# Decaying attention and two feed-forward layers: two more jobs through the DMA crossbar, merged scale passes, and a new order of the first loads

## The chip, the cores and the metric

The kernel runs on one core of one Trainium2 chip. The metric is the device time of one execution in microseconds, as the median of several runs.

## The reference, cut to what matters

```python
# q, k, v: 4 x 8 x 576 x 64; f: 4 x 8 x 576
scores = q @ k.T / 8
cum    = cumsum(log(clip(f, 1e-4, 1)))
attn   = softmax(where(causal, scores + cum[i] - cum[j], -1e9))
x = (attn @ v) as 2304 tokens x 512
h = x @ w_in;  x = (h * sigmoid(h)) @ w_out        # 512 -> 2048 -> 512
h = x @ w2_in; out = (h * cos(h)) @ w2_out         # 512 -> 2048 -> 512
```

All of it is float32.

## The kernel before

**The work.** The 32 heads go in 16 pairs, n = 0 to 15. Each pair has a job "a" for its first 256 rows and a job "b" for its last 320 (`ORDER`). A job "a" is one unit, c01, and a job "b" is three: c3, c2 and T. A unit makes scores on TensorE (PE), subtracts the maximum on VectorE (DVE), takes the exponential on ScalarE (ACT), normalises, transposes the probabilities, and multiplies them by the values (`pv_tasks`).

**Two ways to transpose.** In `unit_tasks` and `pv_tasks` a job "b" takes one of two ways by `BY_DMA`. With False, PE transposes float32 blocks (line 810, the narrow one line 813), ACT copies them from PSUM, and the product is float32 (line 948). With True, the probabilities are split into a high and a low fp16 part (`eh`, line 834 for the low one), six DMA transposes write them to `pt` (lines 841 and 844), the values are split too (line 700), and the product is three fp16 passes (line 937). Before the change this is True for 0 to 5, 6, 8, 10, 12 and 14: eleven jobs.

**Decays.** Logarithms are taken and summed once (`d_ln`, `d_scan`, lines 448 to 452). Jobs "a" with n < 4 add them on PE by a matmul (`f_dk`, line 768); the others read them back from DRAM, spread over the partitions.

**The two layers.** Tokens go in nine groups of 256 (j = 0 to 8) and hidden columns in eight pairs p. A step (l, j, p) is a product into `h` (line 1329; for the first group line 1318), elementwise work that leaves g, and a product into `y` (line 1441 in layer 1, line 1220 in layer 2). In layer 1, groups 0 and 1 take the output weights as float32. From group 2 (`J16`) on they are fp16 pairs, which need a scale for each p (`scale_tasks` with kind "o"), and g is made with `rg3`, the result of `f_v1` (line 1044). Layer 2 is fp16 pairs throughout. Its weights are converted while layer 1 runs and go through DRAM; `f_v` makes its factors.

**A scale.** The squares of a tile are summed by ACT (`squares`, line 358), added by DVE (`f_add`, line 425), summed over the partitions by a matmul with ones (line 429), and turned into a power of two and its inverse by three DVE passes (lines 434 to 436). For q and k of a job "b" the same is done in `balance` (lines 593 to 596).

**The order.** A planner (`Scheduler`) runs a model of the engines while the program is built. At each moment an engine takes the ready task with the lowest key whose buffers (`TOK`) are free, and issues it; so every engine gets a fixed list. Layer steps have keys from -1000 and go first. Jobs "a" have keys 0 to 50 or so, jobs "b" follow, six to a job. The first layer's weights have keys 10 to 60, the squares and scales of its output weights `C16 + C161 * p`, the second layer's weights `C2K0 + C2K1 * i`; their loads wait for step `W2N0 + W2N1 * i`. `KO` adds an offset by the kind of task. While the model finds PE idle in the first 60 us, it puts fillers into PE's list (line 410). All loads are issued from SyncE (SP), in the planned order; `QD` and `LOOK` set how far loads run ahead.

Of the kernel before, what the change touches and what calls it, by code (L numbers as in the profile page):

```python
# [29 lines left out]
BY_DMA = [n < 6 or n % 2 == 0 for n in range(NP)]  # L30
# [25 lines left out]
KO = {"gs": 1.5, "g2": 1.5, "gl2": 1.5, "cb2": 0.5, "cb3": 0.5, "chi": -2.5, "g": -5.5}  # L56
HAM = 3.4133
# [3 lines left out]
EXTRA = {"DVE": 1.2, "POOL": 0.8}  # L61
# [7 lines left out]
KDEC, KDP = 12.0, -0.5  # L69
# [10 lines left out]
class Scheduler:  # L80
# [35 lines left out]
    def run(self):  # L116
# [56 lines left out]
        while events:  # L173
# [23 lines left out]
            while progress:  # L197
                progress = False
                for e in ENG:
# [41 lines left out]
                    if e == "PE":  # L241
                        w = int(now / HAM)
                        while win < w:
                            warm = work[win] > 0.7 * HAM
                            win += 1
                            if len(work) <= win:
                                work.append(0.0)
                        if not warm:
                            end += best.dur
                        a = now  # L250
                        while a < end - 1e-9:
                            w = int(a / HAM + 1e-9)
# [58 lines left out]
def c_dma(mb):  # L311
    return 0.01 + mb / 0.41
# [3 lines left out]
def decay_attention_silu_cos_kernel(ctx, tc, qa, qb, f, w1i, w1o, w2i, w2o, out):  # L316
# [81 lines left out]
    qe = sb.tile([128, 4], I32, name="qe")  # L398
# [20 lines left out]
    def scale_tasks(i, deps, key, top=15, turns=None):  # L419


        cell = {}

        def f_add():
            nc.vector.scalar_tensor_tensor(sq16[:, i:i + 1], sq[:, 0, i:i + 1], 2.0 ** -60, sq[:, 1, i:i + 1], ALU.max, ALU.add)

        def f_sum():
            cell["n"] = ps.tile([128, 512], F32, tag="s", bufs=TOK["s"], name="nrm")
            nc.tensor.matmul(cell["n"][:, 0:1], ones16, sq16[:, i:i + 1], start=True, stop=True, skip_group_check=True)

        def f_two():
            n = cell["n"][:, 0:1].bitcast(I32)
            a, b = scl[:, i:i + 1].bitcast(I32), inv[:, i:i + 1].bitcast(I32)
            nc.vector.tensor_scalar(b, n, 1, 0x3F800000, ALU.logical_shift_right, ALU.bitwise_and)  # L434
# [4 lines left out]
        t = add("DVE", 0.1, f_add, deps, key=key, name="sc")  # L439
        t = add("PE", 0.04, f_sum, [t], key=key - 10000.0, acq=["s"], name="sc")  # L440
        return add("DVE", 0.46, f_two, [t], key=key, rel=["s"], name="sc")
# [5 lines left out]
    def d_ln():  # L447
        nc.vector.tensor_scalar(fc[0:32, 0:S], fc[0:32, 0:S], 1e-4, 1.0, ALU.max, ALU.min)

    def d_scan():  # L450
        nc.vector.tensor_tensor_scan(cum[0:32, 0:S], ones[0:32, 0:S], lf[0:32, 0:S], 0.0, ALU.mult, ALU.add)
        nc.vector.tensor_scalar(cum[0:32, 0:S], cum[0:32, 0:S], -8.0, None, ALU.mult)
# [52 lines left out]
    for i in range(2 * NF):  # L505
# [5 lines left out]
        def load(c=c, kind=kind, src=src):  # L511
# [5 lines left out]
                         [decay] if kind == "o" and c >= NF - NT_ else [], kind == "o")  # L517
# [37 lines left out]
    def load_tasks(jb, u):  # L555
# [5 lines left out]
        def tile_of(tag):  # L561
            n, dt = {"qk": (QK, F32), "v": (QB - RB, F32), "dk": (QB, F32)}[tag]
            if beta:
                return sbt(tag, [128, n], dt, name=tag)
            if not half:
                pairs[tag, jb.n // 2] = sbt(tag, [128, n], dt, name=tag)
            return pairs[tag, jb.n // 2]
# [36 lines left out]
        def norm():  # L604
            jb.qn = ps.tile([128, 512], F32, tag="s", bufs=TOK["s"], name="nrm")
            nc.tensor.matmul(jb.qn[:, 0:nq], ones16, qn.bitcast(BF16).rearrange("p n (c t) -> p n c t", t=2)[:, jb.n, 0:nq, 1], start=True, stop=True, skip_group_check=True)
# [45 lines left out]
        own = beta or not half  # L652
        t0 = add("SP", 0.5, load, key=u, acq=["qs"] if beta else ["qk"] if own else [],
                 deps=[] if own else [jb.mate.loads[2]], dma=c_dma(0.49 if beta else 0.26), name="ldq")
        tv = add("SP", 0.5, load_v, key=u + 0.1, acq=["v"] if own else [], deps=[] if own else [jb.mate.loads[0]],
# [47 lines left out]
        if not beta and jb.n < NS_:  # L703
            if half:
                values.append([tv, jb.mate.loads[0]])
            jb.loads, jb.masked = [tv, tv, t0], {"c01": [masked]}
            return [tl]
        t1 = add("SP", 0.5, decays, [decay] + ([] if own else [jb.mate.loads[1]]), key=u, acq=["dk"] if own else [],
                 dma=1.3 if beta else 1.1, name="ldd")
        jb.loads = [tv, t1, t0]  # L710
# [334 lines left out]
    factors1 = add("DVE", 0.9, f_v1, sc1 + [wready[1, "i", 2 * p][0] for p in range(NPR)], key=-500, name="sc")  # L1045
# [4 lines left out]
    for i in range(2 * NF):  # L1050
# [17 lines left out]
        ts = scale_tasks(k, [halves[c - 1][2], halves[c][2]], key, *((15, by) if kind == "i" else (14,)))  # L1068
# [45 lines left out]
    factors2 = add("DVE", 0.6, f_v, sc2, key=-500, name="sc")  # L1114
# [47 lines left out]
    def factor_tasks(l, j, ts, key):  # L1162
# [20 lines left out]
        if j < 2:  # L1183
            return [add("DVE", 0.1, f1(p, p + 1), [ts, wts[p]], key=key, name="sc") for p in range(NPR)]
        t = add("DVE", 0.1, f1(0, NPR), [ts] + wts, key=key, name="sc")
# [331 lines left out]
```

## Time and profile before

| | |
|---|---|
| median of 3 runs | 912.09 us (912.05 to 913.18) |
| profiled execution | 911.74 us, of which the span of instructions is 909.9 |
| PE busy | 899.1 us, 99% |
| DVE, ACT, POOL busy | 760.6, 694.9, 160.7 us |
| mean granted TensorE clock | 0.996 |

POOL is GpSimd. An engine's busy time counts its own instructions; a matmul's time in the trace includes its way through the array, so that single matmuls overlap. The chain of waits gives each piece of time to one instruction only, and is the better view of what PE's work costs.

### The profile page before, as it was taken

The page shows a single profiled execution, that of the slowest core. Times are in us where ns is not written, and L with a number is a line of the kernel's source. Part 1 is how long each engine was busy: PE and PEld are TensorE (multiplying, and loading weights), DVE is VectorE, ACT ScalarE, POOL GpSimd, SP SyncE. Part 2 cuts the span into 40 slices and gives each one's busy share as a digit, 9 for nine tenths or more (in the row PEclk, how much of TensorE's full clock was granted, in tenths as well). Part 3 has the DMA queues.
Part 4 walks back from the last instruction along what each step waited for, and adds up shares of the span by engine and source line. Part 5 has one row for each costly group of instructions (what it writes and reads, how often), then busy time and mean ns, then how long its engine had stood idle before and what let it go on. Part 6 is the DMA issues. An engine that isn't in the chain of part 4 may idle for free.

```text
span 909.9 us, 20973 instructions
## 1 busy us (share of the span) xinstructions
PE 899.1 (99%) x7928; PEld 753.0 (83%) x7928; DVE 760.6 (84%) x1854; ACT 694.9 (76%) x1425; POOL 160.7 (18%) x236
## 2 busy tenths in 40 slices
PE   9999999999999999999999999999999999999997
PEld 5667777788887888887888888888888888888886
DVE  6899878987876999988899987888888888787775
ACT  7999999876868888788797767766676666666663
POOL 6652321133212324323120100000000000000000
PEclk9999999999999999999999999999999999999999
DMA  8965744967987878886674997000001000000010
GB/s 318 372 223 160 235 151 82 196 142 162 202 191 204 213 215 209 209 191 177 221 233 157 317 355 237 24 24 24 24 24 48 24 24 24 1 25 24 1 24 24
DMA packets 113701, 130.03 MB, mean 143 GB/s; under 512 B 63872, under 2 KB 76160, under 8 KB 113600
## 3 DMA queue, kind: packets, MB, share of 16 engines
q1 hardware_dynamic: 113600, 128.70, 49.2%
q8 instruction: 62, 1.02, 0.5%
q14 instruction: 39, 0.32, 0.1%
HBM read 90.25 MB, written 24.72 MB: 126 GB/s over the span
## 4 chain that ended last, share of the span: by engine, by line
PE 93%; ACT 3%; DVE 2%; DMA 1%; issue 1%; DVEq 0%; ACTq 0%; SPq 0%
PE h L1329 40%; PE y L1441 20%; PE y L1220 18%; PE pv L948 2%; PE spin L410 2%; PE st L762 2%; PE tt L810 2%; PE pv L937 2%; PE st L755 1%; ACT junk L358 1%; PE st L743 1%; PE st L768 1%; DMA rw<-w1i 1%; PE st L742 1%; PE h L1318 0%
## 5 line engine op out<-in xcount | busy, mean ns | idle before, releaser
L1329 PE MATMUL h<-x,wi 128*128 128x256 f16 x3432 | 404.6, 273 | 0.0
L1329 PEld LDWEIGHTS <-wi 128*128 128x128 f16 x3432 | 331.6, 98 | 46.6 <-issue 6.5
L1441 PE MATMUL y<-g,rw 128*128 128x256 f16 (+1 forms) x1600 | 224.1, 292 | 2.7 <-ACT g L333 2.7
L1220 PE MATMUL y<-wo,g 128*128 128x256 f16 x1512 | 176.5, 273 | 0.0
L1220 PEld LDWEIGHTS <-g 128*128 128x128 f16 x1512 | 147.9, 98 | 17.1
L1441 PEld LDWEIGHTS <-rw 128*128 128x128 f16 x1344 | 129.2, 98 | 18.3 <-issue 3.3
L793 ACT ACTIVATE e<-e,su 128x128 f32<-128x128 f32 (+4 forms) x144 | 82.9, 578 | 14.4 <-DVE su L772 14.2
L1383 ACT ACTIVATE t<-h,ru 128x512 f32<-128x512 f32 x72 | 49.2, 684 | 57.8 <-PE h L1329 57.5
L1408 DVE TENSOR_TENSOR g<-t,g 128x896 f16<-128x896 f32 x72 | 78.4, 1089 | 14.9 <-ACT g L1405 13.1
L1405 ACT ACTIVATE g<-t 128x896 f16<-128x896 f32 x72 | 68.0, 944 | 28.8 <-DVE t L1399 28.7
L1393 DVE SCALAR_TENSOR_TENSOR t<-h,rg,t 128x512 f32<-128x512 f32 x72 | 54.0, 749 | 34.7 <-ACT t L1390 34.7
L1389 ACT ACTIVATE t<-t,ru 128x512 f32<-128x512 f32 x72 | 51.7, 717 | 26.7 <-DVE t L1386 26.7
L1354 ACT ACTIVATE t<-h,rg 128x512 f32<-128x512 f32 x72 | 48.9, 680 | 29.3 <-PE h L1329 28.9
L333 ACT ACTIVATE g<-t,rg 128x512 f16<-128x512 f32 (+1 forms) x72 | 51.6, 716 | 22.2 <-PE y L1441 19.4
L772 DVE CUSTOM_DVE_ANT_0 e<-st,dk 128x256 f32<-128x256 f32 (+3 forms) x128 | 59.2, 492 | 8.4 <-PE st L762 3.3
L1386 DVE SCALAR_TENSOR_TENSOR t<-t,ru,h 128x512 f32<-128x512 f32 x72 | 53.5, 743 | 8.9 <-ACT t L1383 8.9
L1357 DVE SCALAR_TENSOR_TENSOR t<-t,h 128x512 f32<-128x512 f32 x72 | 49.2, 683 | 11.9 <-ACT t L1354 11.6
L1441 PEld LDWEIGHTS y<-g,rw 128*128 128x128 f32 x256 | 47.0, 194 | 13.1 <-ACT g L333 3.9
L353 DVE SCALAR_TENSOR_TENSOR g<-t,rg,g 128x512 f16<-128x512 f32 x56 | 43.3, 773 | 13.4 <-ACT g L333 12.8
L1390 ACT ACTIVATE t<-t,halfpi 128x512 f32<-128x512 f32 x72 | 52.0, 722 | 2.3
L834 DVE SCALAR_TENSOR_TENSOR eh<-e,su,eh 128x512 f16<-128x512 f32 (+1 forms) x66 | 41.6, 657 | 1.1 <-ACT eh L333 0.6
L333 ACT ACTIVATE e<-e,su 128x256 f32<-128x256 f32 (+4 forms) x78 | 35.2, 509 | 0.9 <-DVE inv L434 0.5
(158 smaller groups left out, 1260.7 us busy)
## 6 DMA issues: line engine op xcount, KB each, us to landing
rw<-w1i SPq DMA_DIRECT2D x16, 512.0 KB, 5.4
rw<-w1o SPq DMA_DIRECT2D x16, 512.0 KB, 7.3
x<-x_d SPq DMA_DIRECT2D x16, 512.0 KB, 4.2
dk<-decay_d SPq DMA_DIRECT2D x16, 512.0 KB, 4.9
raw<-w2i SPq DMA_DIRECT2D x16, 512.0 KB, 5.0
raw<-w2o SPq DMA_DIRECT2D x16, 512.0 KB, 4.2
qs<-qb SPq DMA_DIRECT2D x16, 480.0 KB, 4.2
w2o_d<-w SPq DMA_DIRECT2D x24, 256.0 KB, 3.3
```

The lines of the kernel that those rows point to most:

```text
L333: nc.scalar.activation(dst, src, AF.Copy, scale=scale)
L772: nc.vector.tensor_tensor_reduce(out, s, d, -0.125, first, ALU.add, ALU.min, cell["sm"][:, o:o + 1])
L793: nc.scalar.activation(x, x, AF.Exp, bias=sm[:, i:i + 1], scale=-1.0, accum_out=sm[:, 4 + i:5 + i])
L1220: nc.tensor.matmul(y[bank][:, 256 * half:256 * half + 256], g[:, gi, ga], w[:, wi, 256 * col:256 * col + 256], start=p == 0 and half == 0 ...
L1329: nc.tensor.matmul(h[:, i], w[:, wi, 128 * k:128 * k + 128], x[:, xi, k], start=(i == 0 and q == 0 and k == 0), stop=(i == 1 and q == 2 an ...
L1386: nc.vector.scalar_tensor_tensor(cell["t"], cell["t"], r, cell["h"], ALU.subtract, ALU.subtract)
L1389: nc.scalar.activation(cell["t"], cell["t"], AF.Abs, scale=r)
L1390: nc.scalar.activation(cell["t"], cell["t"], AF.Sin, scale=-2.0 * PI, bias=halfpi)
L1393: nc.vector.scalar_tensor_tensor(cell["t"], cell["h"], r, cell["t"], ALU.mult, ALU.mult)
L1405: nc.scalar.activation(g_t[s][:, 0], cell["w"], AF.Copy)
L1408: nc.vector.tensor_tensor(g_t[s][:, 1], cell["w"], g_t[s][:, 0], ALU.subtract)
L1441: nc.tensor.matmul(y[:, e * TB:(e + 1) * TB], w[:, wi, 128 * ec:128 * ec + 128], g[:, gi, i * TB:(i + 1) * TB], start=(st and e == 0), sto ...
```

## The change

Two more jobs "b", 7 and 9, take the way through the crossbar. The scales of the first layer's output weights are made for four p at once, and some inverses are made later, all eight of a kind in one pass. `balance` has two passes instead of three; its sum on PE writes the two norms twice. The decays are summed in two parts, and the four matmuls of line 768 wait for the first alone. The loads of a job "a" wait only for the buffer of their pair, and no longer for the load of its other half. `GAPB` puts the jobs "b" 12 key units later, `LEAD` their loads 3 before, `USTEP` their three units 1 apart and not 2. Many constants of the planner have new values.

```diff
-BY_DMA = [n < 6 or n % 2 == 0 for n in range(NP)]
+BY_DMA = [n < 11 or n % 2 == 0 for n in range(NP)]
-LOOK = 12
+LOOK = 14
-QD = 3
+QD = 1.5
-CK2 = 12
+CK2 = 6
-GAP4, GAP8 = 8, 12
+GAP4, GAP8 = 6, 12
-C2K0, C2K1 = 150, 0.5
-W2N0, W2N1 = 30, 1.0
-J16, C16, C161 = 2, 70, 2.0
+C2K0, C2K1 = 160, 0.2
+W2N0, W2N1 = 35, 0.9
+J16, C16, C161 = 2, 90.0, 4
-KO = {"gs": 1.5, "g2": 1.5, "gl2": 1.5, "cb2": 0.5, "cb3": 0.5, "chi": -2.5, "g": -5.5}
-HAM = 3.4133
+KO = {"gs": 0.5, "g2": 1.5, "gl2": 1.5, "cb2": 2.0, "cb3": 0.0, "chi": 2, "g": -8, "max": -0.5, "ldq": 1.0, "exp": -0.5, "xc": -2.0, "nm": 0.0, "rec": -4, "clo": -1.0, "ws": -2.0, "qhi": -1.5, "sqw": -2.5, "cb1": 4, "ldd": -3.0, "hide": -1.0, "tc": 1.5, "vhi": 3.5, "cexp": 0.5}
+HAM, HAM0 = 3.4133, 1.3
-EXTRA = {"DVE": 1.2, "POOL": 0.8}
+EXTRA = {"DVE": 1.2, "POOL": 1.4}
-KDEC, KDP = 12.0, -0.5
+KDEC, KDP = 14, -1
+LEAD, USTEP, GAPB = 3, 1, 12
...
+    def inverse(i, n, top):
+        b = inv[:, i:i + n].bitcast(I32)
+        nc.vector.tensor_scalar(b, b, 1.0, float((65 - top) << 23), ALU.mult, ALU.add)
-    def scale_tasks(i, deps, key, top=15, turns=None):
+    def scale_tasks(i, deps, key, top=15, turns=None, n=1, late=False):
...
-            nc.vector.tensor_scalar(b, b, 1.0, float((65 - top) << 23), ALU.mult, ALU.add)
+            if not late:
+                inverse(i, n, top)
...
+    def d_scan(a, b):
+        def f():
+            nc.vector.tensor_tensor_scan(tot[0:32, a:b], ones[0:32, a:b], lf[0:32, a:b],
+                                         tot[0:32, a - 1:a] if a else 0.0, ALU.mult, ALU.add)
+            nc.vector.tensor_scalar(cum[0:32, a:b], tot[0:32, a:b], -8.0, None, ALU.mult)
+        return f
...
+    d1 = add("DVE", 0.45, d_ln(0, 256), [d0], key=-100)
+    d2 = add("ACT", 0.4, d_log(0, 256), [d1], key=-100)
+    d1 = add("DVE", 0.55, d_ln(256, S), [d1], key=-99)
+    scanned = add("DVE", 0.9, d_scan(0, 256), [d2, dm, dz], key=-100)
+    d2 = add("ACT", 0.5, d_log(256, S), [d1, d2], key=-100)
...
+    d3 = add("DVE", 1.15, d_scan(256, S), [d2, scanned], key=-99)
-    scanned = d3
...
+            nc.vector.scalar_tensor_tensor(qsc[:, :, n].bitcast(I32), qe[:, 1:nq + 1:nq - 1], float(127 << 23), qe[:, 0:2],
+                                           ALU.add, ALU.subtract)
...
-        t0 = add("SP", 0.5, load, key=u, acq=["qs"] if beta else ["qk"] if own else [],
-                 deps=[] if own else [jb.mate.loads[2]], dma=c_dma(0.49 if beta else 0.26), name="ldq")
+        at = {}
+        if not beta:
+            at = jb.mate.at if half else {tag: add("SP", 0.0, lambda: None, key=u - 300, acq=[tag], name="at")
+                                          for tag in (["qk", "v", "dk"] if jb.n >= NS_ else ["qk", "v"])}
+            jb.at = at
+        t0 = add("SP", 0.5, load, key=u, acq=["qs"] if beta else [], deps=[] if beta else [at["qk"]],
+                 dma=c_dma(0.49 if beta else 0.26), name="ldq")
...
-            sp = load_tasks(jb, pos)
+            if kind == "b" and jb.n == 0:
+                pos += GAPB
+            sp = load_tasks(jb, pos - (LEAD if kind == "b" else 0))
...
-                    un += unit_tasks(jb, u, pos + 2 * i, sp, [])
+                    un += unit_tasks(jb, u, pos + USTEP * i, sp, [])
...
+    NQ = 4
...
+        if p % NQ == 0:
+            q = [add(**squares(lambda c=c: wo32[c]["w"], 512, sq[:, c % 2, k + c // 2 - p:k + c // 2 - p + 1]),
+                     deps=wready[1, "o", c], key=C16 + C161 * (c // 2), name="sqw") for c in range(2 * p, 2 * p + 2 * NQ)]
+            ts = scale_tasks(k, q, C16 + C161 * (p + NQ - 1), 14, n=NQ, late=True)
+            sc1.append(ts)
...
+        inverse(o, NPR, 14)
...
+        inverse(i, NPR, 15)
+        inverse(o, NPR, 14)
```

## Rows read from the trace of the kernel before

In the groups of instructions a row has the line, engine and operation, out<-in and the count, then busy us, mean ns of one, and idle us of the engine before them with what ended it. A timeline row has its start and length in us, then the same, and in brackets the idle time before it. In rows 1 a stretch and its length stand first, then the busy time of PE, PEld (its weight loads), DVE, ACT and POOL, each with its count of instructions, the granted clock as a share of 2.4 GHz, the mean busy share of the DMA engines, and GB/s.

**Rows 1.** Busy time of each engine, TensorE's granted clock and DMA, by stretch.

```profile
0.00:60.00 60.00, 58.94 (x380) 37.03 (x381) 47.47 (x143) 52.87 (x155) 39.70 (x55) 1.00 0.91 330
60.00:75.00 15.00, 11.33 (x70) 8.56 (x69) 14.41 (x40) 14.87 (x41) 3.91 (x5) 0.89 0.53 161
75.00:200.00 125.00, 125.00 (x942) 98.50 (x940) 107.70 (x337) 114.50 (x296) 30.45 (x46) 1.00 0.63 159
200.00:440.00 240.00, 240.00 (x2289) 195.11 (x2288) 204.99 (x555) 193.61 (x434) 71.35 (x113) 1.00 0.79 195
440.00:560.00 120.00, 119.59 (x1102) 105.72 (x1101) 102.14 (x240) 90.77 (x177) 15.30 (x19) 1.00 0.79 269
```

**Rows 2.** Groups of TensorE matmuls: fillers, and the sums of squares.

```profile
L410 PE MATMUL spin<-ones 128*128 128x512 bf16 x89 | 24.3, 410 | 1.1 <-DVE ones L372 1.1
...
L429 PE MATMUL nrm<-sq,ones 128*128 128x1 bf16 x50 | 8.4, 168 | 1.4 <-DVE inv L434 1.0 <-DVE sq L425 0.3
```

**Rows 3.** Chain of waits, start and length of each piece in us.

```profile
1.06 5.02 PE spin L410 x12
...
6.93 2.05 PE spin L410 x9
...
70.15 4.54 PE y L1441 x12
...
97.74 2.59 PE y L1441 x12
```

**Rows 4.** Chain of waits, jobs 8 and 9 of the last rows.

```profile
319.12 0.87 PE tt L810 x8
...
322.69 1.80 PE pv L937 x30
...
329.77 2.35 PE pv L948 x20
```

**Rows 5.** Groups of VectorE instructions: low parts of eh and of the values, inverses.

```profile
L834 DVE SCALAR_TENSOR_TENSOR eh<-e,su,eh 128x512 f16<-128x512 f32 (+1 forms) x66 | 41.6, 657 | 1.1 <-ACT eh L333 0.6 <-POOL eh L335 0.5
...
L700 DVE SCALAR_TENSOR_TENSOR pt<-v,scl,pt 128x512 f16<-128x512 f32 (+1 forms) x22 | 11.6, 568 | 0.3 <-ACT pt L333 0.3
...
L436 DVE TENSOR_SCALAR inv<-inv 128x1 int32<-128x1 int32 x50 | 7.7, 153 | 1.7
```

**Rows 6.** Line 844, crossbar transposes: ns min/median/max, and landing.

```profile
L844 SPq DMA_TRANSPOSE pt<-eh x44: 1209/1243/2914, 141.8 to 427.8; - x44
...
DMA to landing us min/median/max: 2.7/3.4/6.7
```

**Rows 7.** Timeline, the decays' first and last pass.

```profile
2.73 0.94 DVE L448 TENSOR_SCALAR fc<-fc 32x576 f32<-32x576 f32 x1 [1.24 <-DMA fc<-f]
...
6.00 0.45 DVE L452 TENSOR_SCALAR cum<-cum 32x576 f32<-32x576 f32 x1
```

**Rows 8.** Timeline of ScalarE and TensorE before the stall.

```profile
63.70 0.63 ACT L358 ACTIVATE junk<-rw 128x512 bf16<-128x512 f32 x1
...
65.60 0.61 PE L1329 MATMUL h<-x,wi 128*128 128x256 f16 x4
...
67.60 0.66 ACT L1354 ACTIVATE t<-h,rg 128x512 f32<-128x512 f32 x1
```

**Rows 9.** Timeline of VectorE and TensorE: scales, last job, seam of the layers.

```profile
177.91 0.23 DVE L1044 TENSOR_SCALAR rg<-v,vm 128x8 f32<-128x8 f32 x1
...
184.46 0.75 DVE L353 SCALAR_TENSOR_TENSOR g<-t,rg,g 128x512 f16<-128x512 f32 x1 [0.72 <-ACT g L333]
...
193.72 0.82 PE L1441 MATMUL y<-g,rw 128*128 128x256 f16 x6
...
443.75 2.42 PE L948 MATMUL pv<-pt,v 128*64 128x320 f32 x20
...
554.30 1.09 DVE L1408 TENSOR_TENSOR g<-t,g 128x896 f16<-128x896 f32 x1 [1.08 <-ACT g L1405]
...
557.46 1.47 PE L1220 MATMUL y<-wo,g 128*128 128x256 f16 x12
```

More of the change, by code (lines that the diff above doesn't have):

```diff
@@ L241, in run @@
                     if e == "PE":
-                        w = int(now / HAM)
+                        w = int((now + HAM0) / HAM)
                         while win < w:
@@ L427, in f_sum @@
         def f_sum():
             cell["n"] = ps.tile([128, 512], F32, tag="s", bufs=TOK["s"], name="nrm")
[L429 removed]
+            nc.tensor.matmul(cell["n"][:, 0:n], ones16, sq16[:, i:i + n], start=True, stop=True, skip_group_check=True)
         def f_two():
[L432 to L434 removed]
+            m = cell["n"][:, 0:n].bitcast(I32)
@@ L440, in scale_tasks @@
         t = add("PE", 0.04, f_sum, [t], key=key - 10000.0, acq=["s"], name="sc")
-        return add("DVE", 0.46, f_two, [t], key=key, rel=["s"], name="sc")
+        return add("DVE", 0.31 if late else 0.46, f_two, [t], key=key, rel=["s"], name="sc")
     fc, lf, ones, cum = [sb.tile([128, 1024], F32, tag=f"wo{NF - NT_ + i}", bufs=1, name=n)
                          for i, n in enumerate(("fc", "lf", "ones", "cum"))]
-    def d_ln():
-        nc.vector.tensor_scalar(fc[0:32, 0:S], fc[0:32, 0:S], 1e-4, 1.0, ALU.max, ALU.min)
@@ L516, in decay_attention_silu_cos_kernel @@
                          dict(rel=["raw"]) if kind == "i" else dict(rel=["lo"]), [],
-                         [decay] if kind == "o" and c >= NF - NT_ else [], kind == "o")
+                         [decay] if kind == "o" and (c >= NF - NT_ or c == NF - NT_ - 2) else [], kind == "o")
         if kind == "o" and c >= NF - NT_ - 1:
@@ L564, in tile_of @@
                 return sbt(tag, [128, n], dt, name=tag)
-            if not half:
+            if (tag, jb.n // 2) not in pairs:
                 pairs[tag, jb.n // 2] = sbt(tag, [128, n], dt, name=tag)
@@ L605, in norm @@
             jb.qn = ps.tile([128, 512], F32, tag="s", bufs=TOK["s"], name="nrm")
-            nc.tensor.matmul(jb.qn[:, 0:nq], ones16, qn.bitcast(BF16).rearrange("p n (c t) -> p n c t", t=2)[:, jb.n, 0:nq, 1], start=True, stop=True, skip_group_check=True)
+            n = qn.bitcast(BF16).rearrange("p n (c t) -> p n c t", t=2)[:, jb.n, 0:nq, 1]
+            nc.tensor.matmul(jb.qn[:, 0:2 * nq], ones16, n.unsqueeze(1).to_broadcast([128, 2, nq]), start=True, stop=True,
+                             skip_group_check=True)
         def rows(a, heads, count, copies):
@@ L650, in decayt @@
                 nc.sync.dma_start(jb.dt[64 * a:64 * a + 64], rows(a, 1, S, 64))
-        own = beta or not half
-        t0 = add("SP", 0.5, load, key=u, acq=["qs"] if beta else ["qk"] if own else [],
-                 deps=[] if own else [jb.mate.loads[2]], dma=c_dma(0.49 if beta else 0.26), name="ldq")
-        tv = add("SP", 0.5, load_v, key=u + 0.1, acq=["v"] if own else [], deps=[] if own else [jb.mate.loads[0]],
+        at = {}
[5 more added lines that the diff above has]
+                 dma=c_dma(0.49 if beta else 0.26), name="ldq")
+        tv = add("SP", 0.5, load_v, key=u + 0.1, acq=["v"] if beta else [], deps=[] if beta else [at["v"]],
                  dma=c_dma(0.33 if beta else 0.13), name="ldq")
@@ L704, in load_tasks @@
             if half:
-                values.append([tv, jb.mate.loads[0]])
-            jb.loads, jb.masked = [tv, tv, t0], {"c01": [masked]}
+                values.append([tv, jb.mate.tv])
+            jb.tv, jb.masked = tv, {"c01": [masked]}
             return [tl]
-        t1 = add("SP", 0.5, decays, [decay] + ([] if own else [jb.mate.loads[1]]), key=u, acq=["dk"] if own else [],
+        t1 = add("SP", 0.5, decays, [decay] + ([] if beta else [at["dk"]]), key=u, acq=["dk"] if beta else [],
                  dma=1.3 if beta else 1.1, name="ldd")
-        jb.loads = [tv, t1, t0]
         r = [tl, tv, t1]
@@ L1044, in f_v1 @@
         nc.vector.tensor_scalar(rg3, v1[:, 1], vm[:, 2:3], 2.0 ** -16, ALU.mult, ALU.mult)
-    factors1 = add("DVE", 0.9, f_v1, sc1 + [wready[1, "i", 2 * p][0] for p in range(NPR)], key=-500, name="sc")
+    factors1 = add("DVE", 1.05, f_v1, sc1 + [wready[1, "i", 2 * p][0] for p in range(NPR)], key=-500, name="sc")
     w2_done = {}
@@ L1067, in decay_attention_silu_cos_kernel @@
         by = sq2[:, p:p + 1] if kind == "i" else scl[:, k:k + 1]
-        ts = scale_tasks(k, [halves[c - 1][2], halves[c][2]], key, *((15, by) if kind == "i" else (14,)))
+        ts = scale_tasks(k, [halves[c - 1][2], halves[c][2]], key, *((15, by) if kind == "i" else (14,)), late=True)
         sc2.append(ts)
@@ L1113, in f_v @@
         nc.vector.tensor_scalar(rg2, v2[:, 1], vm[:, 0:1], 2.0 ** -16 / INV2PI, ALU.mult, ALU.mult)
-    factors2 = add("DVE", 0.6, f_v, sc2, key=-500, name="sc")
+    factors2 = add("DVE", 1.2, f_v, sc2, key=-500, name="sc")
     steps = {}
@@ L1183, in factor_tasks @@
         if j < 2:
-            return [add("DVE", 0.1, f1(p, p + 1), [ts, wts[p]], key=key, name="sc") for p in range(NPR)]
-        t = add("DVE", 0.1, f1(0, NPR), [ts] + wts, key=key, name="sc")
+            return [add("DVE", 0.2, f1(p, p + 1), [ts, wts[p]], key=key, name="sc") for p in range(NPR)]
+        t = add("DVE", 0.2, f1(0, NPR), [ts] + wts, key=key, name="sc")
         return [t] * NPR
```

34 lines of the change are left out of this document (14 added, 20 removed).

## The prediction

> **What bounds the kernel now.** I read the busy time by stretch first [rows 1]. The reader is to see that TensorE (PE) has 125.00 of 125 us from 75 to 200, 240.00 of 240 to 440 and 119.59 of 120 to 560, at a granted clock of 1.00. There the kernel is as long as PE's work. VectorE (DVE) and ScalarE (ACT) are close behind: between 75 and 560 DVE idles 17.3 + 35.0 + 17.9 = 70 us, ACT 10.5 + 46.4 + 29.2 = 86 us.
>
> The first 75 us are different. PE counts as busy in most of them, but 89 of its matmuls are filler, line 410 [rows 2]. In the chain of waits [rows 3] the first twelve take 5.02 us, before any data has landed; 77 more at 2.05 / 9 = 0.23 us make 17.5. From 60 to 75 PE has 11.33 of 15 us at a clock of 0.89 [rows 1]: 3.67 us idle. The twelve matmuls that follow take 4.54 us, where twelve such take 2.59 later [rows 3]: 1.95 us more, at the lower of the two levels of the clock (1.2 instead of 2.4 GHz), after PE had stood. So the head holds 5.0 us of filler that nothing can remove, and 17.5 + 5.6 us that a better order could.
>
> What the change can do is therefore: take work from PE, shorten the head, or bring a wait into the dense part. The sum goes by the profiled execution, 911.74 us (the span of 909.9 and 1.84 around it). The median of the runs shown is 0.35 above it.
>
> **The change part by part.**
>
> *Two more jobs through the crossbar (7 and 9).* Job 9 as it is has 8 + 6 + 4 transposes and a narrow one on PE at 0.87 / 8 = 0.109 us, 2.07 us, and 2.35 us for the float32 product of probabilities and values [rows 4]. A job that goes through the crossbar has no transposes on PE and 1.80 us for the same product in three fp16 passes. The scores are alike. So 2.07 + 2.35 - 1.80 = 2.62 us for each job, in a stretch where PE has no gap: **-5.2 us** for two. If anything else were due there it would be DVE. It gains the low parts, 41.6 / 11 = 3.8 us of eh and 11.6 / 11 = 1.05 us of the values in each job [rows 5], 10 us in all with the values' scales. SP gains 12 transposes of 1.24 us [rows 6], 15 us of its queue in which loads of the next jobs and of x stand behind them. From 200 to 440 PE had no gap beside the transposes of nine such jobs, so I cost that at nothing; without this cover a transpose would show its 3.4 us to landing.
>
> The Trainium skill, "VectorE: DVE Perf Modes", section "Rules for kernel authors", speaks against this edit: a 128x128 transpose goes to TensorE if a result in PSUM will do, otherwise to the DMA crossbar; its table has 390 ns against 1309 ns. The trace agrees that one is dearer on the new path (0.109 us of PE against 1.24 us of SP and 3.4 us to landing). By that rule alone the edit would lose; the sum goes by the engine that is full, and that is PE. The rule's case is the last rival below.
>
> *Small passes merged.* The eight scales of the first layer's output weights become two sets of four: six sums on PE fewer, each between nothing and 0.168 us [rows 2], 0 to 1.0; I take **-0.4**. On DVE three one-column passes go six times, line 436's inverse goes 24 times and returns three times for eight columns, and the balance of q and k has two passes where it had three, in 16 jobs: 18 + 21 + 16 = 55 passes at about the 0.153 us of line 436 [rows 5], 8.4 us. Against the 10 us of the edit before, DVE carries some 2 us more, beside 70 us of idle time: nothing. Without that room it would be those 2 us.
>
> *Log decays in two parts.* Four passes over 576 columns run one after the other from 2.73 to 6.45 [rows 7]. Over the first 256 columns (44%) they take some 1.8 us with their hand-overs: ready at about 4.6. On PE the first scores end at 6.93, and the matmul that adds the decays starts after nine fillers, 2.05 us later [rows 3]. Job 0 can be that much sooner. What is left of it at 75 is unsure, since the DMA share of the first 60 us is 0.91 [rows 1] and the weights have to land as well. Bounds 0 and 2.05; I take **-1.0**.
>
> *First jobs' loads, and the order of the head.* The second job of a pair no longer waits for the first one's load; that goes with the decays. The loads of the last rows' jobs start 12 key units later (GAPB), and the squares of the first layer's output weights get keys 20 to 34 units higher. What this can give is seen before the stall: line 1354 starts at 67.60, though its matmuls end at 66.2, because ACT works through a row of squares. Two of them are of the kinds that move away; the one of an output weight stands at 63.70 [rows 8], 0.8 us with its read-out. That is 1.6 us of a stall of 3.67, and if PE does not stand, the 1.95 of the slow clock go too. Bounds: all 5.6 gone, or a second stall like it (+5.6), since the whole order changes; I take half, **-2.8**. For the other fillers: DMA at 0.91 and ACT at 52.87 of 60 us leave little room. A third fewer is -5.8, nine more are +2.05; I take 0.
>
> *The seam between the layers.* The second layer's weights are converted while the first layer runs. The first g of layer 2 is ready at 554.30 + 1.09 = 555.4, its product runs at 557.46 [rows 9]: 2.1 us of margin. The edits above bring PE there 5.2 + 0.4 + 1.0 + 2.8 = 9.4 us sooner, so the conversion must come 7.3 us sooner, and DVE, which does much of it, is at 102 of 120 us. The last rows' jobs end sooner by about as much as PE saves, so most should follow. Two inverses of eight columns now come just ahead of the factors, some 0.3 us. Bounds 0 and +7.3; I take **+1.5**, nearer to the low end, as DVE and ACT have 18 and 29 us of idle time from 440 to 560.
>
> *Other constants* (LOOK, QD, the offsets of keys, EXTRA, the planner's clock window) change only the order; they stand in the bounds of the head and the seam. CK2 is read for no weight, since W1 = 32.
>
> Sum: -5.2 - 0.4 - 1.0 - 2.8 + 1.5 = -7.9; 911.74 - 7.9 = 903.84, and with 0.35 for the median **904.2 us**.
>
> **The rivals.**
>
> *The head opens (15%).* Decays 2.05, the stall with its slow clock 5.6, 2.5 of the fillers, nothing lost at the seam: 912.09 - 5.2 - 0.4 - 2.05 - 5.6 - 2.5 = 896.3. For it: ACT's squares stand just where PE starves. Against: DMA and ACT are nearly full in the first 60 us.
>
> *The seam takes it back (20%).* PE waits for layer 2's first g, up to 7.3 us: 912.09 - 9.4 + 7.3 = 910.0; with half of that wait 906.3. For it: the margin of 2.1 us, and the last weight's load now waits for step 62 where it waited for 61. Against: DVE's and ACT's idle time there.
>
> *The output weights' scales come late (13%): slower.* Today rg is ready at 177.91, the first g made with it ends at 184.46 + 0.75 = 185.2, and the product that needs this runs at 193.72 [rows 9]: 8.5 us of slack. With the change the second set of four is due at key 118, where the last pair was at 84, and the last rows' jobs, which compete, start at 62 instead of 52: it stands (118 - 62 - 84 + 52) / 6 = 4 jobs later in the line. Job 9's product is at 329.77 [rows 4], job 15's at 443.75 [rows 9], 19 us a job. One and a half jobs late are 28.5 us, less the slack 20: 904.2 + 20 = 924. It turns the sign from 8.5 + 7.9 = 16.4 us of lateness on. Against: by its key the last pair stood behind five jobs, and it was done at 177.91, when by that pace one product had run; low keys are served early, in gaps.
>
> *The crossbar holds the two jobs (5%).* Six transposes of 1.24 us and a landing of 3.4 make 10.8 us between the last low part and the product. If PE waited for that in both jobs: 904.2 + 21.7 = 926. Against: no gap of PE beside nine jobs of that kind.
>
> **How the numbers follow.** Forecast 47%, rivals 15, 20, 13 and 5%. The forecast's own range is 900 to 908. About 0.2%, 1.8 us, is what a measurement of this kernel can tell from no change, so 910.3 to 913.9 is "same". Faster: 47 + 15 + 15 (of the seam's 20) = 77%. Same: the seam's other 5 and 2 of the last rival, 7%. Slower: 13 + 3 = 16%. All good ends together give 912.09 - 5.2 - 1.0 - 2.05 - 5.6 - 5.8 = 892.4. The range goes from 894 to 913, which leaves out the slower cases and a few per cent below.
>
> **What would show each step.** Transposes on PE 186 - 36 = 150 and records of the fp16 product 30 x 13 = 390; the first decay matmul near 7; PE without a gap and at a clock of 1.00 from 60 to 75, or another stall there; the first g with rg ahead of its product; at the seam no gap of PE over 1 us. Wrong would be a gap of PE over 8 us between 130 and 220, clearly more fillers than 89, or a dense part that has not become some 5 us shorter although the two jobs have moved.

## The result, and the profile after

The kernel after the change takes 904.58 us (median of 4 runs, 904.26 to 905.51), the kernel before 912.31 beside it. The ratio is 0.9915 with an interval of 0.9898 to 0.9932: 7.7 us less, where 7.9 was forecast. The profiled execution took 904.74 us with a span of 902.9, which is 7.0 below the span of before. Line numbers of the kernel after are 1 to 26 higher.

Busy time by stretch, after; the columns are those of [rows 1].

```profile
0.00:60.00 60.00, 56.38 (x367) 35.30 (x369) 46.46 (x146) 53.69 (x158) 38.16 (x53) 1.00 0.97 336
60.00:75.00 15.00, 12.45 (x83) 9.61 (x80) 13.53 (x45) 14.87 (x44) 4.73 (x5) 1.00 0.42 138
75.00:200.00 125.00, 124.27 (x949) 97.40 (x948) 109.96 (x330) 120.24 (x313) 21.16 (x36) 1.00 0.68 171
200.00:440.00 240.00, 239.66 (x2308) 196.79 (x2306) 209.96 (x554) 200.35 (x445) 42.30 (x81) 1.00 0.84 202
440.00:560.00 120.00, 119.50 (x1103) 106.41 (x1102) 106.42 (x247) 94.95 (x178) 5.15 (x5) 1.00 0.79 272
```

Beside [rows 1], PE is busy 2.6 us less from 0 to 60 (gaps that are new), 1.1 us more from 60 to 75, and the granted clock is 1.00 there, not 0.89. ACT is nearly full from 75 to 200: 120.24 of 125 us. DVE has hardly changed, though 12 low parts more go through it.

The groups that answer to [rows 2, 5], and two more of PE's:

```profile
L852 DVE SCALAR_TENSOR_TENSOR eh<-e,su,eh 128x512 f16<-128x512 f32 (+1 forms) x78 | 48.2, 646 | 2.6 <-ACT eh L334 2.3
...
L955 PE MATMUL pv<-pt 128*64 128x320 f16 (+2 forms) x390 | 24.3, 270 | 0.0
L828 PE MATMUL tt<-ident,e 128*128 128x128 f32 x150 | 23.9, 278 | 1.7 <-ACT e L334 1.0 <-POOL e L336 0.5
...
L411 PE MATMUL spin<-ones 128*128 128x512 bf16 x71 | 19.6, 411 | 1.1 <-DVE ones L373 1.1
...
L434 PE MATMUL nrm<-sq,ones 128*128 128x1 bf16 (+1 forms) x44 | 7.4, 168 | 0.3 <-DVE sq L430 0.2
```

Transposes are 150 and records of the fp16 product 390, as the prediction had them. There are 71 fillers, not 89.

The timeline of PE in the head, after: the first fillers, the decays of the first job (line 786), and the matmuls behind the stall of [rows 3].

```profile
1.05 4.02 PE L411 MATMUL spin<-ones 128*128 128x512 bf16 x9 [1.05 <-DVE ones L373]
5.00 1.44 PE L773 MATMUL st<-qk 64*128 64x128 f32 x8
6.38 1.58 PE L786 MATMUL st<-cum,sel 128*128 128x128 f32 x8
...
68.78 2.83 PE L1466 MATMUL y<-g,rw 128*128 128x256 f32 x12 [1.84 <-ACT g L334]
```

The decays stand right behind the scores, at 6.38; before, nine fillers stood between them, up to 8.98 [rows 3]. The stall at 69 is 1.84 us long, and the twelve matmuls behind it take 2.83 us and not 4.54.

PE's and DVE's timelines that answer to [rows 9], after: the second sum of four scales, the factors of layer 1, the first product with them, job 15's product, the factors of layer 2, and the first two steps at the seam.

```profile
175.04 0.18 PE L434 MATMUL nrm<-sq,ones 128*128 128x4 bf16 x1
...
177.51 0.23 DVE L1067 TENSOR_SCALAR rg<-v,vm 128x8 f32<-128x8 f32 x1
...
195.93 1.47 PE L1466 MATMUL y<-g,rw 128*128 128x256 f16 x12
...
428.05 2.42 PE L966 MATMUL pv<-pt,v 128*64 128x320 f32 x20
...
538.37 0.23 DVE L1138 TENSOR_SCALAR rg<-v,vm 128x8 f32<-128x8 f32 x1
...
550.37 2.78 PE L1354 MATMUL h<-x,wi 128*128 128x256 f16 x24 [0.17 <-DVE t L1418]
552.99 2.46 PE L1245 MATMUL y<-wo,g 128*128 128x256 f16 x21
```

The factors of layer 1 are ready at 177.51 (before 177.91) and nothing waits for them. PE waits 0.17 us at the seam. Job 15's product starts 15.7 us sooner than before, twice what the kernel gained: this is the row that the experiments turn on.

### The profile page after: what moved, and what is told of

Its sections match the earlier page's. It is cut to its first block, busy times and chain, and to the rows that moved or that the text cites. A ratio compares the mean times of both kernels' runs of the same rounds, so it can differ in the third digit from the quotient of the medians.

```text
span 902.9 us, 20874 instructions
## 1 busy us (share of the span) xinstructions
PE 888.9 (98%) x7886; PEld 746.9 (83%) x7886; DVE 762.5 (84%) x1851; ACT 706.4 (78%) x1454; POOL 111.5 (12%) x179
## 3 DMA queue, kind: packets, MB, share of 16 engines
q8 instruction: 62, 1.02, 0.5%
## 4 chain that ended last, share of the span: by engine, by line
PE 75%; DVE 3%; ACT 1%; DMA 1%; issue 1%; SPq 0%; DVEq 0%; ACTq 0%
PE h L1354 35%; PE y L1245 18%; PE y L1466 15%; PE pv L955 2%; PE st L780 2%; PE pv L966 1%; PE tt L828 1%; DMA qs<-qb 1%; DMA w2o_d<-w 1%; PE st L761 1%; DVE w L354 1%; PE st L760 1%; ACT t L1379 0%; DVE g L354 0%; DVE t L1382 0%
## 5 line engine op out<-in xcount | busy, mean ns | idle before, releaser
L1466 PE MATMUL y<-g,rw 128*128 128x256 f16 (+1 forms) x1600 | 221.0, 290 | 3.0 <-ACT g L334 1.8
L1466 PEld LDWEIGHTS y<-g,rw 128*128 128x128 f32 x256 | 45.9, 190 | 10.8 <-issue 2.7
L852 DVE SCALAR_TENSOR_TENSOR eh<-e,su,eh 128x512 f16<-128x512 f32 (+1 forms) x78 | 48.2, 646 | 2.6 <-ACT eh L334 2.3
L334 ACT ACTIVATE eh<-e,su 128x512 f16<-128x512 f32 (+2 forms) x64 | 37.0, 607 | 1.5 <-ACT e L811 0.8
```

The costliest lines, as they stand in the source:

```text
L334: nc.scalar.activation(dst, src, AF.Copy, scale=scale)
L1466: nc.tensor.matmul(y[:, e * TB:(e + 1) * TB], w[:, wi, 128 * ec:128 * ec + 128], g[:, gi, i * TB:(i + 1) * TB], start=(st and e == 0), sto ...
```

## The experiments

The kernels whose names begin with a are the kernel after with one thing taken back or added, those with b the kernel before with one part put in. Their times stand beside runs of the kernel before on the same chip (911.9 to 912.4). The kernel after was not run again beside them; by the ratios, a difference from it comes out within about 1 us of that of the medians given here. In each, the planner makes a new order for everything.

**b_jobs: the kernel before, with the two jobs alone.**

```diff
-BY_DMA = [n < 6 or n % 2 == 0 for n in range(NP)]
+BY_DMA = [n < 11 or n % 2 == 0 for n in range(NP)]
```

> The kernel before with one edit, jobs 7 and 9 through the crossbar; all constants and everything else as before. Theory: PE is full from 75 us on, so the time falls by what these jobs no longer cost PE, 2 x 2.62 = 5.2 us, to about 907, and the first 75 us stay as they were (89 fillers, the stall at 66 to 70). Rival: every edit makes the planner write a new order, and it is the order that counts; then PE gets new gaps and the time lies anywhere between 906 and 916.

Measured: 933.3 us, ratio 1.0229 (1.0215 to 1.0243). It is 21 us slower, where 5 less was expected of the two jobs. PE's timeline in b_jobs, with the idle time before each piece in brackets:

```profile
458.79 2.42 PE L948 MATMUL pv<-pt,v 128*64 128x320 f32 x20
...
467.45 0.18 PE L429 MATMUL nrm<-sq,ones 128*128 128x1 bf16 x1 [1.52 <-DVE sq L425]
477.15 0.18 PE L429 MATMUL nrm<-sq,ones 128*128 128x1 bf16 x1 [9.52 <-DVE sq L425]
478.65 0.16 PE L429 MATMUL nrm<-sq,ones 128*128 128x1 bf16 x1 [1.32 <-DVE sq L425]
480.74 0.16 PE L429 MATMUL nrm<-sq,ones 128*128 128x1 bf16 x1 [1.92 <-DVE sq L425]
481.45 7.77 PE L1329 MATMUL h<-x,wi 128*128 128x256 f16 x48 [0.54 <-ACT x L333]
```

Busy time in two stretches of it, and the group of the small sums:

```profile
460.00:470.00 10.00, 6.11 (x58) 4.70 (x54) 9.85 (x25) 6.22 (x14) 1.35 (x2) 0.93 0.70 200
470.00:480.00 10.00, 0.35 (x2) 0.23 (x3) 7.71 (x21) 6.16 (x16) 1.62 (x3) 0.50 1.02 394
```

```profile
L429 PE MATMUL nrm<-sq,ones 128*128 128x1 bf16 x50 | 8.4, 168 | 17.6 <-DVE sq L425 16.8 <-DVE inv L434 0.8
```

Job 15's product (458.79) starts 15.0 us later than before [rows 9], and PE stands for some 15 us between 466 and 481. The product at 481.45 is the first of token group 7, which needs the rows of the last jobs. Its way shows in the timelines of SP and ACT in b_jobs: SP loads x at 469.66, behind two stores of y; the loads of x take 6.0 to 6.5 us to land, with the DMA share at 1.02; ACT squares x from 476.93 on, behind the squares of a weight at 476.18 that waited 1.59 us for DVE. DVE is busy 9.85 of 10 us from 460 to 470. By ACT's order the sum at 477.15, with the longest wait, is that of this weight of layer 2, and the sums at 478.65 and 480.74 are of x: what stood behind the weight's sum in PE's list was waiting for x as well. The third row is the landing of the loads of line 1191:

```profile
467.76 1.84 SPq L1464 DMA_DIRECT2D x_d<-yo  x2
469.66 1.49 SPq L1191 DMA_DIRECT2D x<-x_d  x2
...
DMA to landing us min/median/max: 6.0/6.2/6.5
```

```profile
476.18 0.63 ACT L358 ACTIVATE junk<-w 128x512 bf16<-128x512 f32 x1 [1.59 <-DVE w L492]
...
476.93 0.63 ACT L358 ACTIVATE junk<-x 128x512 bf16<-128x512 f32 x1
```

So there is a second bound that the dense rows of PE hide: the line of last-rows jobs, that is, the jobs "b" one behind the other through DVE, ACT, SP and PE. Its end must come some 20 us before PE has used up the groups that are ready.

**a_jobs11: the kernel after, with eleven such jobs.**

```diff
-BY_DMA = [n < 11 or n % 2 == 0 for n in range(NP)]
+BY_DMA = [n < 6 or n % 2 == 0 for n in range(NP)]
```

> The changed kernel with eleven jobs through the crossbar as before (7 and 9 on PE again), the rest as changed. Theory: 5.2 us more than the changed kernel, about 909.8, with its head (71 fillers) unaltered. Rival: the head gave the whole gain, then 904.6; or DVE, which has 10 us less to do here, was what made the seam tight, then the time is between 904.6 and 909.

Measured: 909.91 us, ratio 0.9972 (0.9962 to 0.9983): 5.3 above the kernel after. PE is busy 893.3 us there and 888.9 in the kernel after, with the same 71 fillers: the two jobs are 4.4 us of PE's work. The spans of the two profiles differ by 5.1; the other 0.7 is idle time. Job 15's product stands where it stood:

```profile
428.56 2.42 PE L966 MATMUL pv<-pt,v 128*64 128x320 f32 x20
```

The same edit is worth -5.3 us in one order of the work and +21 in the other. The starts of the products on PE, in us, show where the line of jobs is late (from the timelines; each begins the last work of its job):

| | job 0 | job 6 | job 7 | job 8 | job 9 | job 15 |
|---|---|---|---|---|---|---|
| before | 165.51 | 278.50 | 290.47 | 322.62 | 329.70 | 443.75 |
| b_jobs | 167.18 | 286.36 | 302.76 | 331.33 | 347.08 | 458.79 |
| a_jobs11 | 150.54 | 263.40 | 273.42 | 303.92 | 311.03 | 428.56 |
| after | 151.60 | 266.23 | 282.91 | 303.33 | 325.97 | 428.05 |

In both pairs job 7's product comes 9 to 12 us later by the crossbar, and job 9's 15 to 17. Of the 12 in b_jobs, 7.9 stand at job 6 already, which the edit leaves alone, so part of the delay is the new order. In the kernel after the line has it back by the next job (303.3 and 303.9); in the kernel before it never has. What the crossbar itself adds to a job shows at job 7 in b_jobs, with the last low parts, the last transposes and the product:

```profile
291.42 1.47 DVE L834 SCALAR_TENSOR_TENSOR eh<-e,su,eh 128x384 f16<-128x384 f32 x3
...
294.22 2.94 SPq L841 DMA_TRANSPOSE pt<-eh  x2
...
302.76 1.87 PE L937 MATMUL pv<-pt 128*64 128x320 f16 x30
```

From the end of the last low part to the product it is 9.9 us, about the 10.8 that the last rival reckoned. PE has no gap there: the delay falls on the line and not on PE.

**b_jobs_knobs: b_jobs with three of the new constants.**

```diff
+LEAD, USTEP, GAPB = 3, 1, 12
...
+            if kind == "b" and jb.n == 0:
+                pos += GAPB
-            sp = load_tasks(jb, pos)
+            sp = load_tasks(jb, pos - (LEAD if kind == "b" else 0))
...
-                    un += unit_tasks(jb, u, pos + 2 * i, sp, [])
+                    un += unit_tasks(jb, u, pos + USTEP * i, sp, [])
```

> The kernel before with jobs 7 and 9 through the crossbar and, of the constants, only LEAD 3, USTEP 1 and GAPB 12. With the two jobs alone it took 933.3 us: job 15's product ran at 458.8 instead of 443.75 and PE stood from 466 to 481 for the x of group 7. Theory: the line of the last rows' jobs has become the bound there, and these three constants, which put a job's units closer and its loads ahead, bring it forward: job 15's product before 446, no gap of PE over 2 us at 460 to 485, time 906 to 909. Rival: the line is set by something else (the other constants' weights order, DVE's load without merged passes): still over 920, with the gap.

Measured: 924.25 us, ratio 1.0137 (1.012 to 1.0154). Job 15's product starts at 452.69, and the first product of group 7 still waits:

```profile
470.26 0.18 PE L430 MATMUL nrm<-sq,ones 128*128 128x1 bf16 x1 [1.46 <-DVE sq L426]
471.75 0.16 PE L430 MATMUL nrm<-sq,ones 128*128 128x1 bf16 x1 [1.31 <-DVE sq L426]
472.79 3.40 PE L1332 MATMUL h<-x,wi 128*128 128x256 f16 x12 [0.87 <-ACT x L334]
```

Nine of the 21 us are back, with 6 us of the line. These three alone don't make the room. PE stands for 5.4 us from 440 to 500, and for 6.2 from 340 to 440, where it was 2.0 in b_jobs; the longest wait there is 3.4 us, ahead of a job's transposes.

**a_noknobs: the kernel after, with the old values of the three.**

```diff
-LEAD, USTEP, GAPB = 3, 1, 12
+LEAD, USTEP, GAPB = 0, 2, 0
```

> The changed kernel with LEAD 0, USTEP 2 and GAPB 0, the rest as changed. Theory: the line of the last rows' jobs is later, job 15's product at 438 or more instead of 428; group 7 starts on PE near 459, so up to 15 us of it are covered: 904.6 to 910. Rival 1: the line is as long as in the two-jobs experiment, then 915 or more with a gap of PE at 455 to 480. Rival 2: the line is set by other constants, then 904.6 with job 15 at 428.

Measured: 908.96 us, ratio 0.9968 (0.9957 to 0.998): 4.4 above the kernel after. Job 15's product is at 431.24, only 3.2 us later, where 438 or more was expected. The loss is idle time of PE, most of it in small waits from 500 to 560 (56.38 of 60 us busy); the largest is at the seam:

```profile
552.41 5.40 PE L1354 MATMUL h<-x,wi 128*128 128x256 f16 x48 [1.68 <-DVE t L1418]
```

**b_consts: the kernel before, with every new constant**, these three among them, and the rest of the change left out.

```diff
-LOOK = 12
+LOOK = 14
-QD = 3
+QD = 1.5
...
-J16, C16, C161 = 2, 70, 2.0
+J16, C16, C161 = 2, 90.0, 4
...
-KDEC, KDP = 12.0, -0.5
+KDEC, KDP = 14, -1
+LEAD, USTEP, GAPB = 3, 1, 12
```

> The kernel before with the new constants of the planner alone (keys' offsets, C16, GAPB, LEAD, USTEP, QD, LOOK, EXTRA, the window's phase); eleven jobs, no merged passes, one scan, loads chained as before. Theory: only the head changes; fewer fillers and no slow clock after a stall, 2 to 3 us less than before, about 909.5. Rival: the constants were fitted to the merged passes and the earlier loads, and without them bring waits: 912 or more.

Measured: 915.97 us, ratio 1.0038 (1.0026 to 1.0051). Job 0's product starts at 151.64 and job 15's at 435.04: the constants give the line its room. PE is idle for 5.3 us up to 60 and for 2.1 from 75 to 200, where it was 1.1 and nothing before. Part of what the constants cost shows in the head, where the second job of the first pair waits for its chained load, and the matmuls behind it run at the lower clock (2.89 us for 8, where 8 such take 1.58 at 6.38 in the kernel after):

```profile
10.12 0.93 PE L756 MATMUL st<-qk 64*128 64x128 f32 x8 [1.97 <-DMA qk<-qa]
10.98 2.89 PE L769 MATMUL st<-cum,sel 128*128 128x128 f32 x8
```

**a_oldconsts: the kernel after, with every old constant** (the diff the other way round).

> The changed kernel with the old constants of the planner: thirteen jobs, merged passes, scan in two parts and earlier loads stay. Theory: -5.2 for the jobs, -0.4 for six sums fewer, up to -2 for the decays: 904.7 to 906.7. Rival: the head's gain comes from the constants, which keep squares out of ScalarE's list there, and the scan gives nothing: 906.7; if the old order starves PE with the new passes, over 908.

Measured: 919.96 us, ratio 1.0083 (1.0071 to 1.0096). Job 15's product starts at 449.25, and the stall of the head is worse than before:

```profile
60.00:75.00 15.00, 7.04 (x45) 4.50 (x45) 13.49 (x42) 14.78 (x41) 3.38 (x5) 0.84 0.59 176
```

PE has 7.04 of 15 us there. Most of the new idle time is here: PE is idle for 8.0 us from 60 to 75 and 2.8 from 75 to 200, against 2.5 from 440 to 500. The code of the change without its order is slower than the kernel before; so is its order without its code.

**a_nomerge: the kernel after, with scales and inverses one at a time.**

```diff
-    NQ = 4
+    NQ = 1
...
-            ts = scale_tasks(k, q, C16 + C161 * (p + NQ - 1), 14, n=NQ, late=True)
+            ts = scale_tasks(k, q, C16 + C161 * (p + NQ - 1), 14, n=NQ)
```

> The changed kernel with a scale set for each pair of output weights again, and every inverse made with its scale (the balance of q and k stays at two passes). Theory by the prediction: six sums more on PE, 0.4 us, and 39 small passes more on DVE, hidden: 905.0. Rival: thirteen jobs stand at the edge of the seam, since fourteen brought a gap of 7.7 us there, so 6 us more on DVE show as a gap at 545 to 565 or a later line of jobs: 907 to 911.

Measured: 918.81 us, ratio 1.0072 (1.0059 to 1.0085): 14.2 above the kernel after, where 0.4 was expected of PE and DVE was to hide the rest. The first jobs' products are as in the kernel after up to 123.92 (after: 124.62), but job 0 of the last rows has its product at 162.86 (after: 151.60) and job 15 at 445.10. DVE's busy time between the two, with the columns of [rows 1], first a_nomerge, then after (two of four stretches each):

```profile
110.00:125.00 15.00, 15.00 (x117) 11.63 (x118) 13.49 (x51) 14.97 (x46) 0.71 (x2) 1.00 0.22 61
...
155.00:165.00 10.00, 10.00 (x87) 7.19 (x86) 9.79 (x32) 9.47 (x21) 1.36 (x2) 1.00 0.53 139
```

```profile
110.00:125.00 15.00, 15.00 (x114) 11.49 (x114) 11.21 (x45) 14.97 (x46) 1.36 (x3) 1.00 0.18 53
...
155.00:165.00 10.00, 9.27 (x62) 7.31 (x61) 8.37 (x28) 9.94 (x25) 1.28 (x4) 1.00 0.70 134
```

From 110 to 165 DVE works 50.4 us against 46.6: single scales stand there, ahead of the last rows' jobs. ACT is full in this time in both, 54.2 and 54.8 of 55 us, so it is not shown that DVE is what delays job 0. At group 7 PE then waits as in b_jobs; the group of the sums in a_nomerge has the idle time:

```profile
L434 PE MATMUL nrm<-sq,ones 128*128 128x1 bf16 x50 | 8.4, 168 | 9.6 <-DVE sq L430 8.7 <-ACT pt L334 0.8
```

**a_chain: the kernel after, with the loads of a pair chained as before.**

```diff
-        at = {}
-        if not beta:
-            at = jb.mate.at if half else {...}
-            jb.at = at
-        t0 = add("SP", 0.5, load, key=u, acq=["qs"] if beta else [], deps=[] if beta else [at["qk"]],
+        own = beta or not half
+        t0 = add("SP", 0.5, load, key=u, acq=["qs"] if beta else ["qk"] if own else [],
+                 deps=[] if own else [jb.mate.loads[2]],
```

> The changed kernel with the loads of a pair's second job chained to the first one's again, as before. In the kernel before with the new constants alone, job 1's scores waited 1.97 us for their q and k, until 10.12, and the decays' matmuls after them took 2.89 us at the lower clock level. Theory: the same comes back here and the head loses 2 to 4 us: 906.6 to 908.6. Rival: only job 1 is late and the head is set by the weights' conversion: within 1 us of 904.6.

Measured: 917.04 us, ratio 1.0052 (1.004 to 1.0064): 12.5 above the kernel after, three times what was expected at most. In the head it shows 1.5 us of waiting for a load; most is at group 7 again (job 15 at 440.33):

```profile
460.19 0.16 PE L434 MATMUL nrm<-sq,ones 128*128 128x1 bf16 x1 [1.18 <-DVE sq L430]
464.51 2.90 PE L1351 MATMUL h<-x,wi 128*128 128x256 f16 x12 [4.15 <-ACT x L334]
```

**a_scan1: the kernel after, with the decays summed in one part.**

```diff
-    d1 = add("DVE", 0.45, d_ln(0, 256), [d0], key=-100)
-    d2 = add("ACT", 0.4, d_log(0, 256), [d1], key=-100)
...
+    d1 = add("DVE", 0.95, d_ln(0, S), [d0], key=-100)
+    d2 = add("ACT", 0.7, d_log(0, S), [d1], key=-100)
+    d3 = scanned = add("DVE", 1.95, d_scan(0, S), [d2, dm, dz], key=-100)
```

> The changed kernel with the decays summed in one part, so that the four matmuls of line 768's kind wait for the whole scan. Theory by the prediction: job 0's decays 1.8 us later (near 8.2 instead of 6.4), of which about half is left at 75: 905.1 to 906.4. Rival: PE has fillers to spare there, nothing is left: 904.6.

Measured: 905.43 us (904.0 to 907.23), ratio 0.9925 (0.9913 to 0.9938): 0.85 above the kernel after, which the intervals don't tell from nothing. Its times go with the clock: three of the six executions were granted 0.998 on the mean and took 904.0 to 904.9 us, the other three 0.994 or 0.995 and took 906.0 to 907.2. The profiled one is the slowest, and has the old stall. Job 0's decays start at 6.87, where 8.2 was expected; the kernel after has them at 6.38:

```profile
6.87 2.89 PE L783 MATMUL st<-cum,sel 128*128 128x128 f32 x16
...
70.52 5.46 PE L1463 MATMUL y<-g,rw 128*128 128x256 f32 x12 [3.15 <-ACT g L334]
```

**a_jobs14 and a_jobs16: the kernel after, with fourteen and with all sixteen jobs.**

```diff
-BY_DMA = [n < 11 or n % 2 == 0 for n in range(NP)]
+BY_DMA = [n < 12 or n % 2 == 0 for n in range(NP)]
```

(a_jobs16: True for every n.)

> The changed kernel with job 11 through the crossbar as well, fourteen jobs. Theory: PE loses another 2.6 us and the jobs' line (product of job 15 at 428, x of group 7 loaded 15 us ahead) has room: 902. Rival: DVE's 5 us more for a job make the line or the seam late: 904 to 912.

> The changed kernel with all sixteen jobs through the crossbar. Theory, if PE stays the bound: 904.6 - 3 x 2.62 = 896.7. Rival: three jobs bring 15 us more to DVE, at 106 of 120 us in 440 to 560, and each crossbar job lengthens the line of jobs by several us, as 7 and 9 did alone: job 15's product after 440, a gap of PE at group 7 or at the seam, 905 to 925. I take the rival for likelier.

Measured: 910.12 us, ratio 0.9982 (0.9973 to 0.999), and 926.39, ratio 1.0165 (1.015 to 1.0179). With fourteen, job 15 (430.12) still has room, but layer 2's factors come at 545.44 (after: 538.37), and PE waits for them at the seam:

```profile
552.23 4.32 PE L1354 MATMUL h<-x,wi 128*128 128x256 f16 x20 [7.73 <-DVE t L1418]
```

With sixteen, job 15's product is at 445.98, and group 7 waits:

```profile
459.48 0.16 PE L434 MATMUL nrm<-sq,ones 128*128 128x1 bf16 x1 [8.32 <-DVE sq L430]
468.07 0.16 PE L434 MATMUL nrm<-sq,ones 128*128 128x1 bf16 x1 [8.44 <-DVE sq L430]
471.28 0.16 PE L434 MATMUL nrm<-sq,ones 128*128 128x1 bf16 x1 [3.04 <-DVE sq L430]
```

**a14_c2: fourteen jobs, with layer 2's weights converted earlier.**

```diff
-C2K0, C2K1 = 160, 0.2
+C2K0, C2K1 = 146, 0.2
```

> The changed kernel with fourteen crossbar jobs and the second layer's weights converted earlier (C2K0 146 instead of 160). With fourteen jobs alone layer 2's factors came at 545.4 and PE stood 7.7 us at the seam, 910.1. Theory: the conversion had been put behind the last jobs by its key alone; 14 units earlier it is done in time, and PE keeps the third 2.6 us: 902, faster than both kernels. Rival: DVE has no room, and what the conversion gains the jobs' line loses: a gap at group 7 or still at the seam, 906 to 915.

Measured: 925.26 us, ratio 1.0144 (1.0131 to 1.0157). The gap at the seam is gone, and a larger one stands at group 7, since job 15 moved to 453.89 (job 14 stands at 422.30, with fourteen jobs alone at 420.98):

```profile
440.00:500.00 60.00, 38.57 (x332) 31.87 (x332) 52.21 (x129) 51.12 (x107) 1.49 (x2) 0.83 0.71 240
```

What the conversion of the weights gets, the line of jobs lacks. That it is DVE's and ACT's time that they share is argued from this row (52.21 and 51.12 of 60 us, while PE has 38.57), and not shown.

## Why the prediction was right

**The time** came out at -7.7 us for -7.9. In the profiles the span fell by 7.0, and the terms below account for it to 0.6. That the sum lies within 0.2 of the forecast is in part luck: a fall of 4.7 us in fillers, taken at 0, was offset by 2.6 us of new gaps up to 60 and by jobs that took 4.4 us off PE and not 5.2.

- *Two jobs, -5.2.* Right in the kernel after: 5.3 by a_jobs11, of which 4.4 is PE's work. What was wrong is the sentence that costs the crossbar's load on DVE and SP at nothing because PE had no gap beside nine such jobs. A dense PE showed only that the line of jobs was early enough, not by how much. By how much can be read: where PE stood, group 7's first product came 20 to 28 us after job 15's (b_jobs 22.7, a_nomerge 22.2, a_chain 24.2, b_jobs_knobs 20.1, a_jobs16 27.9). Before the change that makes 463.8 to 472 from 443.75 [rows 9], and PE was dense through it: hardly any room. In the kernel after it makes 448 to 456, and PE has work till then. The last rival, at 926 with 5%, had the right sign for the two jobs by themselves (933), with too low a price (21.7 us, where 933.3 lies 26 above the 907 expected) and at the wrong place: PE doesn't wait in the two jobs, but more than 100 us later. The Trainium skill, "VectorE: DVE Perf Modes", section "Rules for kernel authors", which sends such a transpose to TensorE first, agrees with b_jobs (+21 us) and not with the kernel after beside a_jobs11 (-5.3).
- *Merged passes, -0.4.* There are six sums fewer (44 for 50); that PE gains 0.4 by them no run shows. DVE's sum was right: with 8.4 us saved against the new low parts it carries 1.9 us more (762.5 for 760.6), where 2 was reckoned. That this makes "nothing" of the passes was wrong. Taking back most of them costs 14.2 us; the single scales then stand in DVE's list between the first jobs and the last rows'. How much of this is DVE's time and how much the new order that the planner makes, the runs don't separate.
- *Log decays, -1.0.* The decays start sooner (6.38 for 8.98), but hardly by the scan in two parts: with one part they start at 6.87 in a_scan1, so 0.5 of the 2.6 us is the scan's, and the rest comes with other parts of the change. Its worth is 0.85, which can't be told from nothing.
- *Head, -2.8 with fillers at 0.* The twelve matmuls behind the stall take 1.7 us less (2.83 for 4.54), and idle time from 60 to 75 fell from 3.67 to 2.55: of the stall's 5.6 us half went, as taken. Fillers fell by 4.7 us, which was taken at 0, and idle time up to 60 rose from 1.06 to 3.62. That is -5.0 in all, for -3.8 with the decays.
- *Seam, +1.5.* 0.17 us. But idle time of PE from 75 to 560 in all rose by 1.2, and the tail behind PE's last matmul by 0.6.
- *The sum by the profiles*: -4.4 for the jobs, -5.0 in the head, +1.2 and +0.6 of waits make -7.6, for -7.0; +0.6 is not assigned.
- *Scales late (13%)* did not happen: the second set of four was summed at 175.04, the factors were ready at 177.51, and the first product with them ran at 195.93.

So the forecast was right, with a gap in its reasons. The jobs are nearly the only part that shortens PE's dense work; most of the rest of the change (constants, merged passes, free loads) is what makes the line of jobs 15 us earlier (without the constants job 15's product is at 449.25, without the merged passes at 445.10, with the chained loads at 440.33), and without any one of the three groups the kernel after is slower than the kernel before: 919.96, 918.81, 917.04. Their worths don't add up, since each run has a new plan; the last two pay mostly at the same place, group 7, and the first mostly in the head. Thirteen is the edge that the runs found: fourteen jobs lose 7.7 us at the seam. No kernel that was run beats the kernel after.

**Open:** whether the 14 and 12 us of a_nomerge and a_chain come from the edit or from the order that the planner finds with it. An edit in an order that is held fixed was not tried.

## What to carry to other kernels

A full engine tells what the kernel costs now, and not how far the next bound is: find the last result that the full engine needs from the others, here job 15's, and measure the time from it to its first use. An edit that takes work from the full engine and lengthens that line needs its room first; made alone it may lose four times what it gains together with it, as here. An engine's idle time over the kernel doesn't show that work on it is hidden: a_nomerge lost 14 us by passes that the sums had at nothing, with the order that came with them.

## What the runs showed of the hardware

PE's idle time is booked to small instructions: the sums of squares, of 0.17 us each, have 17.6 us of idle time ahead of them in b_jobs, 1.4 before the change [rows 2]. That they cause it doesn't follow: the sum with 9.52 us ahead of it is a weight's, and what came next waited for x. Standing costs twice. From 470 to 480 the granted clock was 0.50 (1.2 GHz), and the 48 matmuls after it took 7.77 us, where 48 such took 5.40 in a_noknobs. After a stall of 1.84 us in the head of the kernel after, the 12 matmuls behind it took 2.83 us; after one of 3.15 us in a_scan1 the same 12 took 5.46, at the lower level.
